# Moving score dots to ScalarE and block updates to VectorE in a residual codebook search

## The chip, the cores and the metric

The kernel runs on one NeuronCore of a Trainium2 chip. The time is the device time of one execution in microseconds. The engines are TensorE (PE, with its weight loads shown apart as PEld), VectorE (DVE), ScalarE (ACT), GpSimd (POOL) and SyncE (SP, which here only issues DMA). Each engine works through its own queue in order; semaphores order the engines among each other. TensorE writes its results to PSUM banks, from which VectorE and ScalarE read.

## The reference

The input is `x` of 2 x 16000 x 512 in bf16. It is a small speech codec: a depthwise convolution of three taps over time, SiLU, four rounds of nearest-codeword search (8 codewords each) on a running residual, and a second depthwise convolution of the chosen codewords' sum.

```python
for i in range(K):                       # K = 3
    z = z + xp[:, i:i+T, :] * dw_enc[i][None, None, :]
z = _silu(z)
res = z
q = jnp.zeros_like(z)
for s in range(Nq):                      # Nq = 4, 8 codewords each
    cb = codebooks[s]
    d2 = einsum(res, res)[..., None] - 2.0 * einsum(res, cb) + einsum(cb, cb)
    idx = d2.argmin(-1)
    sel = cb[idx]
    q = q + sel
    res = res - sel
for i in range(K):
    y = y + qp[:, i:i+T, :] * dw_dec[i][None, None, :]
```

## The kernel before

The 32000 tokens lie as 128 rows of 250 groups, so that one group is 128 tokens, one on each partition. The groups are cut into 17 chunks (`SIZES`, line 27): one of 12, thirteen of 16, two of 12 and one of 6, which is worked on as 8. Channels are on the partitions for most of the work, as four blocks of 128 (`KT` = 4).

For each chunk, `front` runs four blocks. VectorE forms the three tap products (L688) and part of their sums (L696); the other sums are accumulating DMA transfers issued by GpSimd (L694). ScalarE and VectorE alternate for SiLU: exponential (L700), plus one (L704), logarithm (L708), exponential of its negative (L711), and the product into the residual `RES` (L716). `RES` holds the tokens and, between them, columns of the codewords times -2.

Then come four `stage`s, one for each codebook:

- `score` (L769) is TensorE's. For up to six groups at a time it fills one PSUM bank of the pool `psG`, which has two: first a mask (L776), then products of the residual with itself and with the neighbouring codeword columns (L784). The diagonal of the first gives the norm, the columns beside it give eight dots for each token. In a chunk of 16 groups a stage has three such units (6, 6 and 4 groups), in one of 12 two of 6, in the last two of 4: 188 in all.
- `norm` (L804, VectorE) takes the maximum over the masked square, which is the norm. `dots` (L808, VectorE) copies the eight dots of each token from the bank to `PR` and gives the bank back.
- On VectorE the norm is added (L827), then the codewords' norms (L831); the least is taken (L837) and its place marked in the one-hot tile `OH` (L842).
- TensorE turns the one-hots (L853), VectorE copies them (L865), TensorE expands them to pairs (L874), and ScalarE cuts them (`PH`, L883).
- The residual is updated block by block, in one of two ways. For the first `on_dve[s]` blocks TensorE collects the chosen words in `SEL` (`chosen`, L910, six matmuls), and VectorE adds them to `RES` (`subtract`, L920). For the others TensorE builds the whole new residual in `NEW` in two halves (`rest`, L926 and L931), and ScalarE copies each half back (`keep`, L938, or L940 in the smaller chunks). The list `ON_DVE` (line 30) says for each chunk how many blocks of the three updating stages go the first way.

`finish` decodes the one-hots of a chunk into outputs on TensorE (L972); ScalarE copies them out of PSUM (L978), and SyncE issues the stores.

The set-up makes an identity, a mask, the code columns, pair tables and taps. Seven decoder tables are zeroed on VectorE (`taps_of`, L501), filled by DMA from GpSimd's queue (L506) and multiplied by the codewords. Three one-hot tiles are zeroed on VectorE (`presets`, L487). The first chunk's rows are transposed on TensorE (L585) and copied to `XT` for two blocks by ScalarE and for two by VectorE (`move`, L587 to L592).

The order on every engine is written out by a planner (`Plan`, L116). Each piece of work is entered by `plan.add` with its engine, the time it holds it, the time until its result is there, what it needs, a due time, and the slots that it takes and gives (`psG` is the two score banks, `psA` three other PSUM tiles, `Z`, `T`, `E` and so on the SBUF buffers). `run` lists the work forward and backward a few times with shifted ranks (`ROUNDS`) and then shifts ranks by a list of seeds (`MOVES`); the last pass emits the instructions in the order of their planned starts. The planned times order the instructions; on the chip they run when semaphores allow.

Of the kernel before, what the change touches and what calls it, by code (L numbers as in the profile page):

```python
# [14 lines left out]
ACT = mybir.ActivationFunctionType  # L15
# [14 lines left out]
ON_DVE = [(2, 2, 2)] * 3 + [(3, 3, 2)] * 6 + [(3, 3, 3)] * 6 + [(4, 4, 4)] * 2  # L30
# [16 lines left out]
ROUNDS = [(71979, 0.3, 0, 6), (14162, 1, 2, 3), (37709, 0.3, 0, 3), (8398, 0.1, 0.5, 2)]  # L47

MOVES = [403398, 277512, 691281, 942486, 98997, 464427, 609168, 599375, 437497, 903441, 104869, 655643, 319045,
# [59 lines left out]
SWITCH, CLING, SLOW = 0.1, 10.0, 1.08  # L109
# [174 lines left out]
def kernel(  # L284
# [8 lines left out]
    nc = tc.nc  # L293
# [192 lines left out]
    def presets(n):  # L486
        nc.vector.memset(OHB[n], 0.0)  # L487
# [589 lines left out]
```

## Time and profile before

| | |
|---|---|
| median of 3 runs | 682.74 us (680.28 to 682.83) |
| profiled execution | 685.71 us |
| its span, first to last instruction | 683.9 us |
| mean granted TensorE clock | 0.952 |
| busy: VectorE | 637.7 us (93%) |
| busy: ScalarE | 613.0 us (90%) |
| busy: TensorE | 579.5 us (85%) |
| busy: GpSimd | 88.6 us (13%) |

A line of a group says: source line, engine, operation, output <- input with shapes, the number of instructions, then busy time, the mean duration of one in ns, and the engine's idle time just before them with what ended it. Durations of neighbours on one engine overlap, so the distance from one start to the next says what an instruction holds its engine for. In the timeline the columns are start, duration, engine, line, operation. A waits line says who waited for whom, how long in total, how many times, and the longest.

### The profile page before, as it was taken

How to read it: one execution, taken by the hardware profiler on the slowest of the kernel's cores; microseconds unless marked ns; L12 is line 12 of the kernel's file. 1: busy time of each engine (PE TensorE's matmuls, PEld its weight loads, DVE VectorE, ACT ScalarE, POOL GpSimd, SP SyncE). 2: the span in 40 equal slices, each digit the busy share in tenths (PEclk: the TensorE clock that was granted, in tenths of full speed). 3: DMA queues.
4: the chain of work that ended last, by engine and by line, in shares of the span. 5: the costliest groups of instructions: out<-in, count | busy, mean ns of one | idle time of the engine just before them, and what ended most of it. 6: DMA issues, size and time to landing. Idle time of an engine off the chain costs nothing. (4 is left out here: it accounts for less than half of the span.)

```text
span 683.9 us, 25912 instructions
## 1 busy us (share of the span) xinstructions
PE 579.5 (85%) x11637; PEld 332.0 (49%) x11637; DVE 637.7 (93%) x1383; ACT 613.0 (90%) x529; POOL 88.6 (13%) x125
## 2 busy tenths in 40 slices
PE   5056788889989988899888999998988998999995
PEld 5022446454545444454554545554545545556552
DVE  8999999999999989999999999998999999999771
ACT  3589899999999989999999999999999998993556
POOL 6021110110101111110101011101101210010000
PEclk8558899999999999999999999999999999999998
DMA  6999889899698899859898988997679955340335
GB/s 154 179 158 183 151 143 163 167 202 186 126 210 192 150 187 185 186 108 216 211 190 191 170 157 158 192 250 117 146 154 188 187 131 128 97 111 34 126 124 216
DMA packets 162617, 111.55 MB, mean 163 GB/s; under 512 B 143561, under 2 KB 143946, under 8 KB 162378
## 3 DMA queue, kind: packets, MB, share of 16 engines
q1 hardware_dynamic: 150032, 69.88, 45.2%
q0 software_dynamic: 12192, 39.76, 32.3%
q8 instruction: 91, 1.49, 0.9%
q10 hardware_dynamic: 282, 0.26, 0.1%
q14 instruction: 20, 0.16, 0.1%
HBM read 2.39 MB, written 32.77 MB: 51 GB/s over the span
## 5 line engine op out<-in xcount | busy, mean ns | idle before, releaser
L784 PE MATMUL PS<-RES 128*64 128x80 bf16 (+1 forms) x8064 | 175.0, 202 | 10.6 <-DVE RES L716 6.2
L784 PEld LDWEIGHTS <-RES 128*64 128x64 bf16 x8064 | 169.6, 114 | 20.1 <-DVE RES L716 6.8
L920 DVE TENSOR_TENSOR RES<-RES,SEL 128x2048 bf16<-128x2048 bf16 (+2 forms) x183 | 161.3, 910 | 5.4 <-PE SEL L910 5.1
L978 ACT ACTIVATE YSB<-Y 128x1024 bf16<-128x1024 f32 x126 | 127.6, 1037 | 22.8 <-PE Y L972 20.8
L694 POOL DMA_DIRECT2D Z<-T x80 | 73.8, 942 | 510.6 <-DMA XT<-in_x_dram 69.9
L700 ACT ACTIVATE E<-Z 128x2048 bf16<-128x2048 bf16 (+2 forms) x68 | 123.3, 1816 | 9.5 <-DVE Z L696 7.1
L708 ACT ACTIVATE LN<-E 128x2048 f32<-128x2048 bf16 (+2 forms) x68 | 123.1, 1810 | 5.7 <-DVE E L704 4.6
L711 ACT ACTIVATE E<-LN 128x2048 bf16<-128x2048 f32 (+2 forms) x68 | 122.8, 1806 | 0.3
L938 ACT ACTIVATE RES<-NEW 128x1024 bf16<-128x1024 f32 x102 | 104.9, 1053 | 3.6 <-PE NEW L931 3.1
L804 DVE TENSOR_REDUCE TR<-PS 128x6 bf16<-128x384 f32 (+1 forms) x188 | 94.0, 505 | 12.8 <-PE PS L784 12.4
L688 DVE TENSOR_SCALAR T<-XT,WENC 128x2048 bf16<-128x2048 bf16 (+2 forms) x136 | 94.9, 704 | 6.5 <-DMA Z<-T 5.7
L972 PE MATMUL Y<-A,OHT 128*128 128x512 bf16 x249 | 84.6, 386 | 10.3 <-DVE RES L920 5.8
L926 PE MATMUL NEW<-RES,IDENT 128*128 128x512 bf16 (+1 forms) x240 | 71.9, 382 | 10.0 <-ACT RES L938 5.0
L716 DVE TENSOR_TENSOR RES<-Z,E 128x2048 bf16<-128x2048 bf16 (+2 forms) x68 | 77.2, 1136 | 0.2 <-ACT E L711 0.2
L910 PE MATMUL SEL<-PH,HIGH 64*128 64x512 bf16 (+2 forms) x288 | 55.1, 377 | 13.9 <-ACT RES L938 6.0
L776 PE MATMUL PS<-MASK,IDENT 128*64 128x384 bf16 (+1 forms) x376 | 63.3, 333 | 3.6 <-DVE PR L808 3.4
L696 DVE TENSOR_TENSOR Z<-Z,T 128x2048 bf16<-128x2048 bf16 (+2 forms) x56 | 62.5, 1117 | 1.3 <-DMA Z<-T 1.3
L972 PEld LDWEIGHTS <-OHT 128*128 128x128 bf16 x373 | 31.1, 98 | 50.8 <-issue 24.4
L910 PE MATMUL SEL<-PH,MID 64*128 64x512 bf16 (+2 forms) x288 | 52.9, 361 | 0.0
L910 PE MATMUL SEL<-PH,LOW 64*128 64x512 bf16 (+2 forms) x288 | 52.9, 360 | 0.0
L931 PE MATMUL NEW<-PH,EVEN 64*128 64x256 bf16 (+1 forms) x240 | 50.8, 420 | 0.0
L688 DVE TENSOR_SCALAR Z<-XT,WENC 128x2048 bf16<-128x2048 bf16 (+2 forms) x68 | 47.8, 704 | 0.0
(111 smaller groups left out, 617.5 us busy)
## 6 DMA issues: line engine op xcount, KB each, us to landing
Z<-T POOLq DMA_DIRECT2D x65, 512.0 KB, 6.2
out_dram<-YSB SPq DMA_DIRECT2D x61, 512.0 KB, 3.4
Z<-T POOLq DMA_DIRECT2D x10, 384.0 KB, 5.3
RES<-in_x_dram SPq DMA_DIRECT2D x1, 1664.0 KB, 7.2
Z<-T POOLq DMA_DIRECT2D x5, 256.0 KB, 3.7
XT<-in_x_dram SPq DMA_TRANSPOSE x75, 7.1
out_dram<-YSB SPq DMA_DIRECT2D x1, 384.0 KB, 2.4
out_dram<-YSB SPq DMA_DIRECT2D x1, 256.0 KB, 5.4
```

The source lines that it names most:

```text
L688: nc.vector.tensor_scalar(out=places(u[name]), in0=taps(i, k), scalar1=WENC[:, i, k:k + 1], scalar2=None, op0=ALU.mult)
L700: nc.scalar.activation(u["E"][:, 0:G, :], u["Z"][:, 0:G, :], ACT.Exp, scale=-1.0)
L708: nc.scalar.activation(u["LN"][:, 0:G, :], u["E"][:, 0:G, :], ACT.Ln)
L711: nc.scalar.activation(u["E"][:, 0:G, :], u["LN"][:, 0:G, :], ACT.Exp, scale=-1.0)
L716: nc.vector.tensor_tensor(out=tokens(st["RES"], i, G), in0=halves(u["Z"]), in1=halves(u["E"]), op=ALU.mult)
L784: nc.tensor.matmul(V[d * HT:(d + 1) * HT, own - left:own + HT + right], lhsT=row[:, at:at + HT], rhs=row[:, at - left:at + HT + right], st ...
L804: nc.vector.tensor_reduce(out=to, in_=both(u["V", q], m, home, HT), axis=AX.X, op=ALU.max)
L910: nc.tensor.matmul(SEL[:, h, 0:W], lhsT=words[side(h), i * P:(i + 1) * P], rhs=u["PH"][side(h), :], start=(k == 0), stop=(k == len(parts) ...
L920: nc.vector.tensor_tensor(out=old, in0=old, in1=new, op=ALU.add)
L938: nc.scalar.activation(old, new.rearrange("p h (n t) -> p (h n) t", t=HT), ACT.Copy)
L972: nc.tensor.matmul(Y[:, h, :], lhsT=lhs(), rhs=rhs, start=(a == 0), stop=(a == len(terms) - 1))
L978: nc.scalar.activation(u["YSB"][:, k:k + n, :], u[k][:, 0:n, :], ACT.Copy)
```

## The change

Seven things are changed:

- `dots` is a ScalarE copy (an ACTIVATE with Copy) of the same elements from the same bank. It needs the scoring alone, no longer the norm, and the bank is given back when both the norm and the dots are done.
- `ON_DVE` gives 3 blocks of every updating stage to VectorE in chunks 0 to 13 and 4 in chunks 14 to 16. Before, it was 2 in chunks 0 to 2, then (3, 3, 2), then 3, and 4 in the last two chunks.
- All four set-up copies of `move` are ScalarE's.
- `presets` and `taps_of` zero on GpSimd.
- The planner's costs of code columns go from 1.4 (or 1.2) to 0.9, those of the norm from 0.065 to 0.068 a group.
- The planner's costs of TensorE: the turn of one-hots 0.06 to 0.1 (0.13 to 0.1 a tile in the last stage), half a block of `rest` 0.2 to 0.28 plus the same rest, decoding 0.2 to 0.215 a matmul.
- `ROUNDS` and `MOVES`, the seeds, are others, and `MOVES` is longer.

```diff
-ON_DVE = [(2, 2, 2)] * 3 + [(3, 3, 2)] * 6 + [(3, 3, 3)] * 6 + [(4, 4, 4)] * 2
+ON_DVE = [(3, 3, 3)] * 14 + [(4, 4, 4)] * 3
...
-ROUNDS = [(71979, 0.3, 0, 6), (14162, 1, 2, 3), (37709, 0.3, 0, 3), (8398, 0.1, 0.5, 2)]
+ROUNDS = [(46341, 0.3, 0, 4), (76308, 0.1, 2, 3), (32118, 0.1, 0, 1), (72125, 0.1, 0, 1), (12125, 0.3, 0, 1)]
...
     def presets(n):
-        nc.vector.memset(OHB[n], 0.0)
+        nc.gpsimd.memset(OHB[n], 0.0)
...
         t, first, tap, count = PARTS[name]
-        nc.vector.memset(t, 0.0)
+        nc.gpsimd.memset(t, 0.0)
...
-    preset = [plan.add("DVE", 0.3, 0.3 + 0.2, [], early + 2.0 if n == 0 else 0.1 * PERIOD, lambda n=n: presets(n)) for n in range(3)]
+    preset = [plan.add("POOL", 0.5, 0.7, [], early + 2.0 if n == 0 else 0.1 * PERIOD, lambda n=n: presets(n)) for n in range(3)]
...
-            t = plan.add("DVE", 0.2, 0.3, [], (0.3 + 0.02 * n) * PERIOD, lambda name=name: taps_of(name))
+            t = plan.add("POOL", 0.5, 0.7, [], (0.3 + 0.02 * n) * PERIOD, lambda name=name: taps_of(name))
...
-            if i % 2:
-                nc.vector.tensor_copy(st["XT"][:, 0:G + 2, i, :], src)
-            else:
-                nc.scalar.activation(st["XT"][:, 0:G + 2, i, :], src, ACT.Copy)
+            nc.scalar.activation(st["XT"][:, 0:G + 2, i, :], src, ACT.Copy)
...
-            cost = (0.11, 0.07)[i % 2] * (G + 2)
-            st["moved", i] = plan.add(("ACT", "DVE")[i % 2], cost, cost + 0.2, [t], early, lambda i=i: move(i), give=("psA",))
+            cost = 0.11 * (G + 2)
+            st["moved", i] = plan.add("ACT", cost, cost + 0.2, [t], early, lambda i=i: move(i), give=("psA",))
...
-            nc.vector.tensor_copy(to, both(u["V", q], m, code, C).rearrange("p n o c -> p c n o"))
+            src = both(u["V", q], m, code, C).rearrange("p n o c -> p c n o")
+            nc.scalar.activation(to, src, ACT.Copy)
...
-            maxima.append(plan.add("DVE", 0.07 + 0.065 * m, 0.2 + 0.065 * m, [t], due, lambda q=q, m=m: norm(q, m)))
-            maxima.append(plan.add("DVE", 0.06 + 0.01 * m, 0.2, [maxima[-1]], due, lambda q=q, m=m: dots(q, m), give=("psG",)))
+            maxima.append(plan.add("DVE", 0.07 + 0.068 * m, 0.2 + 0.068 * m, [t], due, lambda q=q, m=m: norm(q, m)))
+            maxima.append(plan.add("ACT", 0.11 + 0.007 * m, 0.3, [t], due, lambda q=q, m=m: dots(q, m)))
+            plan.add("FREE", 0.0, 0.0, maxima[-2:], due, lambda: None, give=("psG",))
...
-        hold = 0.13 * MB if last else 0.06
+        hold = 0.1 * MB if last else 0.1
...
-                c = plan.add("PE", 0.2 + 0.65 * f * SLOW, 0.4 + 0.65 * f * SLOW, ready + [st["new"][i, part]], due,
+                c = plan.add("PE", 0.28 + 0.65 * f * SLOW, 0.48 + 0.65 * f * SLOW, ready + [st["new"][i, part]], due,
...
-            d = plan.add("PE", 0.2 * count, 0.2 * count + 0.25, needs, due, lambda k=k: decode(k), take=("psA",))
+            d = plan.add("PE", 0.215 * count, 0.215 * count + 0.25, needs, due, lambda k=k: decode(k), take=("psA",))
```

More of the change, by code (lines that the diff above doesn't have):

```diff
@@ L45 @@
 FAR = -3.3e38
-ROUNDS = [(71979, 0.3, 0, 6), (14162, 1, 2, 3), (37709, 0.3, 0, 3), (8398, 0.1, 0.5, 2)]
-MOVES = [403398, 277512, 691281, 942486, 98997, 464427, 609168, 599375, 437497, 903441, 104869, 655643, 319045,
[55 rows of a table removed]
+ROUNDS = [(46341, 0.3, 0, 4), (76308, 0.1, 2, 3), (32118, 0.1, 0, 1), (72125, 0.1, 0, 1), (12125, 0.3, 0, 1)]
+MOVES = [949848, 17671, 932175, 573655, 719188, 8996, 997728, 468587, 575333, 264370, 591951, 836327, 423319, 577496,
[86 rows of a table added]
 CELLS, COLUMNS, ROWS, QUARTERS = range(4)
@@ L522 @@
     codes = [setup(0.3, 0.5, [ident, book], early, code_words)]
-    codes[0] = plan.add("DVE", 1.4, 1.6, codes, early + 2.0, lambda: code_columns(RESB[0]))
+    codes[0] = plan.add("DVE", 0.9, 1.1, codes, early + 2.0, lambda: code_columns(RESB[0]))
     scored = [plan.add("DVE", 1.3, 1.4, [ident], early + 1.0, mask),
               setup(1.9, 2.1, [ident, book], -0.5 * PERIOD, code_norms)]
-    preset = [plan.add("DVE", 0.3, 0.3 + 0.2, [], early + 2.0 if n == 0 else 0.1 * PERIOD, lambda n=n: presets(n)) for n in range(3)]
+    preset = [plan.add("POOL", 0.5, 0.7, [], early + 2.0 if n == 0 else 0.1 * PERIOD, lambda n=n: presets(n)) for n in range(3)]
     firsts = plan.add("DVE", 1.3, 1.5, [ident], early + 4.0, first_ones)
@@ L534 @@
         words.append(plan.add("DVE", 1.3, 1.5, [t, expanded] + words[-1:], early + 3.0 + s, lambda s=s: pair_words(s)))
-    codes.append(plan.add("DVE", 1.4, 1.6, [codes[0]], 0.1 * PERIOD, lambda: code_columns(RESB[1])))
+    codes.append(plan.add("DVE", 0.9, 1.1, [codes[0]], 0.1 * PERIOD, lambda: code_columns(RESB[1])))
     gate, decoder = [], []
@@ L597, in load_rows @@
                          take=("psA",))
-            cost = (0.11, 0.07)[i % 2] * (G + 2)
-            st["moved", i] = plan.add(("ACT", "DVE")[i % 2], cost, cost + 0.2, [t], early, lambda i=i: move(i), give=("psA",))
+            cost = 0.11 * (G + 2)
+            st["moved", i] = plan.add("ACT", cost, cost + 0.2, [t], early, lambda i=i: move(i), give=("psA",))
             moved.append(st["moved", i])
         st["loaded"] = moved
-        codes.append(plan.add("DVE", 1.2, 1.4, moved + staged + codes[0:1], 0.2 * PERIOD, lambda: code_columns(RESB[2])))
+        codes.append(plan.add("DVE", 0.9, 1.1, moved + staged + codes[0:1], 0.2 * PERIOD, lambda: code_columns(RESB[2])))
         staged.extend(moved)
```

141 rows, old and new, of the table MOVES are left out of this document.

## The prediction

> **What bounds the kernel now.** First the page's head and engine line, then busy time by stretch of the span, then the waits.
>
> ```profile
> span 683.9 us, 25912 instructions
> PE 579.5 (85%) x11637; PEld 332.0 (49%) x11637; DVE 637.7 (93%) x1383; ACT 613.0 (90%) x529; POOL 88.6 (13%) x125
> ```
> ```profile
> 0.00:20.00 20.00, 10.57 (x105) 9.81 (x105) 17.36 (x63) 6.50 (x6) 12.34 (x41) 0.83 0.73 146
> 40.00:60.00 20.00, 13.07 (x147) 6.69 (x147) 19.29 (x38) 18.48 (x17) 2.66 (x3) 0.67 1.08 184
> ...
> 400.00:500.00 100.00, 89.61 (x1853) 50.76 (x1851) 95.91 (x192) 96.07 (x79) 12.60 (x13) 0.97 0.80 167
> 500.00:600.00 100.00, 91.33 (x1964) 53.41 (x1963) 98.06 (x216) 94.72 (x87) 14.82 (x19) 1.00 0.68 151
> 600.00:640.00 40.00, 39.31 (x887) 24.14 (x881) 37.31 (x113) 25.46 (x32) 1.40 (x2) 1.00 0.26 77
> ```
>
> The columns of a stretch are its length, then busy PE, PEld, DVE, ACT and POOL, the granted clock (0.97 to 1.00 late in the span), the DMA share and GB/s. The start is VectorE's. From 400 to 600 VectorE has 194.0 of 200 us and ScalarE 190.8: two engines share the bound, with 6 and 9 us left. From 600 to 640 ScalarE is down to 25.5 of 40, while TensorE has 39.3 and VectorE 37.3. So work taken from VectorE pays everywhere; work put on ScalarE is free only at both ends. What is idle on the two is largely waiting for TensorE:
>
> ```profile
> ACT YSB L978 <- PE Y L972: 20.8, 16, 4.0
> DVE TR L804 <- PE PS L784: 12.4, 16, 2.1
> PEld L776 <- DVE PR L808: 12.4, 22, 1.9
> DVE RES L920 <- PE SEL L910: 5.1, 9, 0.9
> ```
>
> VectorE loses 17.5 us to the scoring and block matmuls; the third row shows the reverse, the next scoring waiting 22 times for a score bank that the dots copy gives back.
>
> **Part 1: dots leave VectorE, blocks come to it.**
>
> ```profile
> L920 DVE TENSOR_TENSOR RES<-RES,SEL 128x2048 bf16<-128x2048 bf16 x105 | 125.9, 1210 | 3.0 <-PE SEL L910 2.9
> L804 DVE TENSOR_REDUCE TR<-PS 128x6 bf16<-128x384 f32 x128 | 69.6, 547 | 7.7 <-PE PS L784 7.5
> L808 DVE CAST PR<-PS 128x48 bf16<-128x48 f32 x128 | 24.8, 196 | 0.0
> L808 DVE CAST PR<-PS 128x32 bf16<-128x32 f32 x60 | 10.7, 179 | 0.0
> ```
> ```profile
> 304.85 1.21 DVE L920 TENSOR_TENSOR RES<-RES,SEL 128x2048 bf16<-128x2048 bf16 x1
> 305.98 0.54 DVE L804 TENSOR_REDUCE TR<-PS 128x6 bf16<-128x384 f32 x1
> ...
> 306.57 0.19 DVE L808 CAST PR<-PS 128x48 bf16<-128x48 f32 x1
> 306.69 0.54 DVE L804 TENSOR_REDUCE TR<-PS 128x6 bf16<-128x384 f32 x1
> ...
> 633.22 1.02 DVE L920 TENSOR_TENSOR RES<-RES,SEL 128x768 bf16<-128x768 bf16 x2
> 634.16 0.26 DVE L837 TENSOR_REDUCE M<-KEY 128x8 bf16<-128x64 bf16 x1
> ```
>
> Rows overlap, so the price of one is the distance to the next start: dots 0.12 us (306.57 to 306.69), a block of a 16-group chunk 1.13, the two halves of a 12-group chunk's block 0.94. Leaving: 128 x 0.12, and 60 x 0.10 for the smaller form, 21.4 us. Coming: the list of blocks sums to 144 before and 162 after, 12 more in 16-group chunks (3 each in chunks 1 and 2, 1 each in 3 to 8) and 6 in 12-group ones (3 each in chunks 0 and 14): 12 x 1.13 + 6 x 0.94 = 19.2. VectorE: **-2.2 us**. By place, chunks 0 to 2 gain VectorE work (3 x 1.13 less 12 x 0.12, some 2 us each), 9 to 13 lose 1.4 each.
>
> **Part 2: ScalarE.**
>
> ```profile
> L938 ACT ACTIVATE RES<-NEW 128x1024 bf16<-128x1024 f32 x102 | 104.9, 1053 | 3.6 <-PE NEW L931 3.1
> L883 ACT ACTIVATE PH<-ps_oh 128x512 bf16<-128x512 f32 x39 | 24.7, 632 | 3.0 <-PE ps_oh L874 3.0
> L940 ACT ACTIVATE RES<-NEW 128x768 bf16<-128x768 f32 x18 | 14.5, 827 | 4.8 <-PE NEW L931 4.7
> L592 ACT ACTIVATE XT<-ps_x 128x1792 bf16<-128x1792 bf16 x2 | 3.3, 1664 | 5.9 <-PE ps_x L585 5.9
> L883 ACT ACTIVATE PH<-ps_oh 128x256 bf16<-128x256 f32 x3 | 1.1, 382 | 0.6 <-PE ps_oh L874 0.6
> ```
> ```profile
> 308.20 0.62 ACT L883 ACTIVATE PH<-ps_oh 128x512 bf16<-128x512 f32 x1
> 308.67 1.05 ACT L938 ACTIVATE RES<-NEW 128x1024 bf16<-128x1024 f32 x1
> 309.58 1.95 ACT L708 ACTIVATE LN<-E 128x2048 f32<-128x2048 bf16 x1
> ```
>
> Each block had two copies here. Leaving: 24 of 0.91 us (308.67 to 309.58) and 12 of about 0.70 (827 ns less the same overlap of 0.14), 30.2 us. Coming: 188 dots, which no row shows on this engine. The two forms of L883 give 0.98 ns an element ((632 - 382) / 256), so a dots of 48 elements would last about 0.18 us by a straight line. If it overlaps as the big ones do, it holds the engine 0.04; if each waits for its matmul and overlaps nothing, 0.18. I take 0.14, nearer the second since each has a TensorE result of its own to await: 188 x 0.14 = 26.3 (ends 7.5 and 34). Two set-up copies come too, 2 x 1.66 less overlap, 3.0. ScalarE: **-0.9 us**, between -20 and +7, not evenly: chunks 9 to 13 get 12 dots each for nothing given back, 1.7 us a chunk.
>
> The Trainium skill, page "ScalarE: Activation LUTs", section "What ACT_TABLE_LOAD costs", gives an ACTIVATE with immediate operands 186 ns plus 0.833 ns an element, and 93 ns of overlap back to back. By it a dots is 0.23 us long and holds the engine 0.13, and the 188 would be 25 us; the rows of 512 and 1024 elements above (632 and 1053 ns) agree with it to 3%, and no run here shows 48 elements.
>
> **Part 3: set-up.**
>
> ```profile
> 24.00 1.08 DVE L590 COPY XT<-ps_x 128x1792 bf16<-128x1792 bf16 x1
> ...
> 25.00 0.60 DVE L688 TENSOR_SCALAR T<-XT,WENC 128x1536 bf16<-128x1536 bf16 x1
> ```
> ```profile
> 6.09 3.92 POOL L451 COPY EXPAND<-LEAST 128x64 bf16<-128x64 bf16 x16 [4.79 <-DVE LEAST L439]
> ...
> 8.07 0.27 DVE L501 MEMSET B<- 128x256 uint32 x1
> ...
> 11.24 0.35 DVE L379 TENSOR_SCALAR CBT<-ps_cbt 128x128 bf16<-128x128 bf16 x2 [0.47 <-PE ps_cbt L377]
> ```
> ```profile
> L501 DVE MEMSET A<- 128x256 uint32 x4 | 1.1, 272 | 0.0
> L633 POOL MEMSET XT<- 128x1024 bf16 x1 | 1.0, 951 | 0.0
> ```
>
> The two XT copies free VectorE of 2 x 1.0 us inside its dense start; ScalarE, busy 6.5 of the first 20 us, hides them, and if it didn't, the fourth block's products would come at most 3.3 us later. Ten memsets of 0.27 (seven tables, three one-hot tiles) are 2.7 us, but the last of them ends at 8.34 us, and at 11.24 VectorE waits for the codebook's transposes anyway: I count 0.5 (ends 0 and 2.7). GpSimd takes them at about half of 951 ns, 4.8 us in all; it idles 4.79 us before its L451 copies. Behind them in its queue stand those copies, the picks, the table fetches and later the accumulating transfers; uncovered, those slip by up to 4.8 us, but the one-hots are first needed when the first score is complete. VectorE: **-2.5 us**.
>
> **Part 4: TensorE, and the new order.**
>
> ```profile
> 308.38 0.39 PE L910 MATMUL SEL<-PH,HIGH 64*128 64x512 bf16 x2 [0.39 <-ACT RES L938]
> ...
> 309.13 0.60 PE L926 MATMUL NEW<-RES,IDENT 128*128 128x512 bf16 x2
> ...
> 310.21 0.60 PE L926 MATMUL NEW<-RES,IDENT 128*128 128x512 bf16 x2
> ```
>
> A block for VectorE costs TensorE 0.75 us (308.38 to 309.13), a block for ScalarE twice 1.08 (309.13 to 310.21). 18 blocks change sides: 12 x 1.41 + 6 x 1.06 = **-23 us** of 579, three blocks of it in chunk 14, near the stretch where TensorE is 98% busy. The planner's cost of a half block was 0.90 and becomes 0.98, nearer to 1.08; decoding goes from 0.20 to 0.215. These are numbers for the planner alone, and with new seeds every engine's order is drawn again. Its worth can only be bounded: between nothing and all of the 17.5 us that VectorE waits for TensorE; the worst, a loss as large, isn't excluded. I take -4: a quarter, since most of TensorE's relief falls on chunks 0 to 2 and 14.
>
> **Part 5: the new waits.** Dots now stand in ScalarE's queue. Behind one that waits for its scoring stand exponentials, logs, block copies and output copies; ahead of it can be an L708 of 1.95 us. The sum of the norms waits for both engines, and so does the bank (two exist): what TensorE lost in 22 waits can grow. The cost is from nothing to half a norm (0.27) on each of 188, 51 us; with a planner that sees these waits I take a tenth of that, **+5**. In the tail the dots lie beside the norms, about -1.
>
> **The sum.** On VectorE -2.2 - 2.5, waits for TensorE -4, new waits +5, tail -1, and 2 to 3 us for ScalarE relieved in chunks 0 to 2 (6 x 0.91 less 1.7, -3.8 a chunk, where its backlog starts): -7. The profiled execution took 685.71 us, 1.8 beyond its span and 3 above the median of 682.74; 682.74 x 678.7 / 685.71 = 675.8, say **676 us**.
>
> **Rivals.** *Nothing gained.* ScalarE becomes the bound in chunks 9 to 13: 190.8 + 5 x 1.7 = 199.3 of the 200 us from 400 to 600. Early relief carries over only through four Z buffers. It gives back 5 to 9 us: 682.
>
> *Norm and dots take turns at a bank.* For it: they read one score bank from two engines, which no row of before shows (PS has L804 and L808 alone, both on VectorE). If the second must wait for the first, whichever engine comes second stands: up to 0.48 us for ScalarE behind a norm, or for VectorE behind a dots that is itself behind a 1.95 us log. The planner gives both the same need, and doesn't know of the turn. Were a third of 188 pairs to collide at 0.3 us, and most of it to show on engines with 3 to 5% to spare, 19 us: 676 + 16 = 692. It decides from 12 us, 0.06 a pair. Against it: both queues are long, so most pairs meet at different times.
>
> The Trainium skill, page "PSUM — Partial Sum Buffer", section "PSUM bank collisions raise a hardware error", speaks for this rival: two engines on one bank and quadrant collide, read against read included, so software has to order them. No row of this trace shows the case.
>
> *The order is much better.* All 17.5 us of VectorE's waits for TensorE go: 665. Against it: the waits shown remain causal, not only badly ordered.
>
> **Chances.** Forecast 0.46 (669 to 680), better order 0.14, nothing gained 0.16, turns at the bank 0.24. What a measurement of this kernel can tell from no change is about 0.5%, 3.4 us: faster 0.59, same 0.15, slower 0.26. The range goes from the better order, 664, to the turns at the bank, 692.
>
> **What would show it.** Right: L808 on ScalarE 188 times at 0.16 to 0.23 us; L920 of 2048 elements 117 times; VectorE near 633 us busy, ScalarE near 612, TensorE near 555; less VectorE waiting for scoring. Wrong: ScalarE idle before dots on VectorE's norms, or VectorE idle before norms and sums on ScalarE's dots, over 12 us together; ScalarE over 99% from 400 to 600; late table fetches.

## The result and the profile after

The changed kernel takes 704.88 us (median; 700.97 to 707.88) against 681.51 us before on the same chip: a ratio of 1.031, 95% interval 1.026 to 1.037. It is 23 us slower where the prediction had 7 us faster, and 13 us above the upper end of the range. Ratios leave out executions over 1.5% above the same kernel's fastest; where times scatter over 20 us that can be half of them or more, so for such kernels the median of all stands beside the ratio.

First the head and the engine line of the page after, to be laid beside the prediction's first fence.

```profile
span 701.1 us, 25688 instructions
PE 564.0 (80%) x11546; PEld 331.0 (47%) x11546; DVE 633.6 (90%) x1207; ACT 606.9 (87%) x683; POOL 92.3 (13%) x135
```

All three large engines have less work than before: VectorE 633.6 us (637.7), ScalarE 606.9 (613.0), TensorE 564.0 (579.5). The span grew by 17.2 us all the same. VectorE's idle time went from 683.9 - 637.7 = 46.2 to 701.1 - 633.6 = 67.5 us: 21.3 more idle, less 4.1 of work, is the 17.2. So none of the three got more work; the added time is idle time. The granted TensorE clock isn't the difference: it was 0.952 in the profiled execution of before and 0.950 in this one.

The groups of instructions, each shape apart, on ScalarE and then on VectorE:

```profile
L837 ACT ACTIVATE PR<-PS 128x48 bf16<-128x48 f32 x128 | 28.1, 221 | 22.2 <-DVE TR L832 15.9 <-PE PS L812 5.6
L837 ACT ACTIVATE PR<-PS 128x32 bf16<-128x32 f32 x60 | 12.5, 210 | 12.8 <-PE PS L812 6.4 <-DVE TR L832 6.3
```
```profile
L950 DVE TENSOR_TENSOR RES<-RES,SEL 128x2048 bf16<-128x2048 bf16 x117 | 140.9, 1219 | 7.3 <-PE SEL L940 7.1
L716 DVE TENSOR_SCALAR T<-XT,WENC 128x2048 bf16<-128x2048 bf16 x104 | 77.5, 751 | 10.9 <-DMA Z<-T 10.9
```

The dots are there 188 times, the large block updates 117 times instead of 105. Behind the bar stands what is new: ScalarE is idle 35.0 us ahead of its dots, nearly as long as the dots themselves last (28.1 + 12.5 = 40.6). The waits of ScalarE and of VectorE (who waited for whom, us in total, times, longest):

```profile
ACT PR L837 <- DVE TR L832: 22.1, 35, 3.4
ACT PR L837 <- PE PS L812: 12.0, 13, 3.3
```
```profile
DVE RES L950 <- PE SEL L940: 12.3, 15, 5.0
DVE T L716 <- DMA Z<-T: 10.9, 3, 7.4
DVE TR L832 <- PE PS L812: 6.6, 12, 1.4
DVE TR L832 <- ACT PR L837: 4.7, 7, 2.3
```

The first row and the last are the turns at a score bank: 35 dots stood behind the norm of the same bank and 7 norms behind the dots, 26.8 us together. VectorE's wait for scoring fell from 12.4 to 6.6 us, but its wait for block matmuls rose from 5.1 to 12.3 and that for accumulating transfers into `Z` from 5.7 (row below) to 10.9. The row of before for that last one:

```profile
DVE T L688 <- DMA Z<-T: 5.7, 5, 2.3
```

How a turn looks in the timeline (start, length, engine, line; in brackets the idle time before it and who ended it). In the first pair the dots wait for the norm, in the second the norm for the dots:

```profile
311.31 0.56 DVE L832 TENSOR_REDUCE TR<-PS 128x6 bf16<-128x384 f32 x1
...
311.90 0.21 ACT L837 ACTIVATE PR<-PS 128x48 bf16<-128x48 f32 x1 [0.43 <-DVE TR L832]
...
319.32 0.25 ACT L837 ACTIVATE PR<-PS 128x48 bf16<-128x48 f32 x1
...
319.61 0.56 DVE L832 TENSOR_REDUCE TR<-PS 128x6 bf16<-128x384 f32 x1 [0.65 <-ACT PR L837]
```

The planner gives the two no order (to it the dots need the scoring alone), yet in neither pair do they run at once: one engine stands until the other has read. That is what the Trainium skill, page "PSUM — Partial Sum Buffer", section "PSUM bank collisions raise a hardware error", demands of software, and the trace agrees: in both brackets the releaser is the other engine's read. Which of the two stands, the order of the program fixes, and not who comes first: in the second pair VectorE stood from 318.96 (319.61 less 0.65), and the dots that it waited for began only at 319.32.

So a turn also hands on whatever made the other engine late. The longest of the 35 waits is of that kind. VectorE had stood 3.38 us for an accumulating transfer, and its norm came late by as much:

```profile
282.78 0.75 DVE L716 TENSOR_SCALAR T<-XT,WENC 128x2048 bf16<-128x2048 bf16 x1 [3.38 <-DMA Z<-T]
...
284.01 0.20 ACT L837 ACTIVATE PR<-PS 128x32 bf16<-128x32 f32 x1 [3.40 <-DVE TR L832]
```

Where the loss sits is seen in busy time by stretch (columns as in the prediction: length, PE, PEld, DVE, ACT, POOL, clock, DMA share, GB/s):

```profile
400.00:500.00 100.00, 81.32 (x1645) 46.85 (x1643) 85.22 (x145) 85.21 (x96) 11.30 (x12) 0.93 0.86 169
500.00:600.00 100.00, 89.12 (x1945) 51.91 (x1941) 97.90 (x182) 94.58 (x113) 13.93 (x18) 1.00 0.63 130
```

From 500 to 600 VectorE is as dense as before (97.9 against 98.1). From 400 to 500 it lost 10.7 us (85.22 against 95.91), half of its 21.3 us of new idle time, and all three engines are less busy there. The timeline there:

```profile
468.82 11.26 SPq L646 DMA_TRANSPOSE XT<-in_x_dram  x4
...
480.88 0.86 POOL L722 DMA_DIRECT2D Z<-T  x1 [14.98 <-DMA XT<-in_x_dram]
...
485.94 0.75 DVE L716 TENSOR_SCALAR T<-XT,WENC 128x2048 bf16<-128x2048 bf16 x1 [7.36 <-DMA Z<-T]
...
487.87 0.61 PE L940 MATMUL SEL<-PH,HIGH 64*128 64x512 bf16 x2 [8.00 <-DVE RES L950]
...
491.42 1.02 ACT L968 ACTIVATE RES<-NEW 128x1024 bf16<-128x1024 f32 x1 [7.70 <-PE NEW L961]
```

GpSimd stood 15 us before its accumulating transfer and was released by the transposing loads of `x`, four of which were issued from 468.82 to 480.08. The transfer was issued at 480.88 and landed some 5 us later; VectorE, next in line for the buffer, stood 7.36 us; TensorE then 8.00 us for VectorE, ScalarE 7.70 for TensorE. One late transfer so holds all three engines in turn, because each queue is in a fixed order. No row of before shows VectorE waiting more than 2.3 us for this transfer.

So two things were on the table: the turns at the bank, which belong to the change, and the order, in which things come late that have nothing to do with dots.

### The profile page after: what moved, and what is told of

The parts are those of the page before. It is cut to its first block, busy times and chain, and to the rows that moved or that the text cites. A ratio compares the mean times of both kernels' runs of the same rounds, so it can differ in the third digit from the quotient of the medians.

```text
span 701.1 us, 25688 instructions
## 1 busy us (share of the span) xinstructions
PE 564.0 (80%) x11546; PEld 331.0 (47%) x11546; DVE 633.6 (90%) x1207; ACT 606.9 (87%) x683; POOL 92.3 (13%) x135
## 5 line engine op out<-in xcount | busy, mean ns | idle before, releaser
L950 DVE TENSOR_TENSOR RES<-RES,SEL 128x2048 bf16<-128x2048 bf16 (+2 forms) x207 | 181.9, 914 | 12.5 <-PE SEL L940 12.3
L812 PE MATMUL PS<-RES 128*64 128x72 bf16 (+1 forms) x8064 | 175.8, 201 | 12.4 <-DVE RES L744 3.9
L716 DVE TENSOR_SCALAR T<-XT,WENC 128x2048 bf16<-128x2048 bf16 (+2 forms) x136 | 96.6, 717 | 10.9 <-DMA Z<-T 10.9
L832 DVE TENSOR_REDUCE TR<-PS 128x6 bf16<-128x384 f32 (+1 forms) x188 | 95.2, 514 | 12.5 <-PE PS L812 6.6
L968 ACT ACTIVATE RES<-NEW 128x1024 bf16<-128x1024 f32 x78 | 79.9, 1034 | 9.5 <-PE NEW L961 9.5
L940 PE MATMUL SEL<-PH,HIGH 64*128 64x512 bf16 (+2 forms) x324 | 63.0, 382 | 27.1 <-DVE RES L950 12.9
L837 ACT ACTIVATE PR<-PS 128x48 bf16<-128x48 f32 (+1 forms) x188 | 39.2, 218 | 35.0 <-DVE TR L832 22.1
L940 PE MATMUL SEL<-PH,MID 64*128 64x512 bf16 (+2 forms) x324 | 61.6, 371 | 0.3 <-DVE MID L510 0.3
L940 PE MATMUL SEL<-PH,LOW 64*128 64x512 bf16 (+2 forms) x324 | 61.2, 369 | 0.3 <-DVE LOW L510 0.3
L956 PE MATMUL NEW<-RES,IDENT 128*128 128x512 bf16 (+1 forms) x168 | 51.4, 388 | 5.9 <-DVE RES L950 3.8
L804 PEld LDWEIGHTS <-IDENT 128*64 128x64 bf16 x376 | 22.9, 108 | 54.7 <-issue 52.6
```

The costliest lines, as they stand in the source:

```text
L716: nc.vector.tensor_scalar(out=places(u[name]), in0=taps(i, k), scalar1=WENC[:, i, k:k + 1], scalar2=None, op0=ALU.mult)
L804: nc.tensor.matmul(both(V[d * HT:(d + 1) * HT], m, home, HT), lhsT=IDENT[:, d * HT:(d + 1) * HT], rhs=MASK[:, 0:m, :].rearrange("p (n o) t ...
L812: nc.tensor.matmul(V[d * HT:(d + 1) * HT, own - left:own + HT + right], lhsT=row[:, at:at + HT], rhs=row[:, at - left:at + HT + right], st ...
L832: nc.vector.tensor_reduce(out=to, in_=both(u["V", q], m, home, HT), axis=AX.X, op=ALU.max)
L940: nc.tensor.matmul(SEL[:, h, 0:W], lhsT=words[side(h), i * P:(i + 1) * P], rhs=u["PH"][side(h), :], start=(k == 0), stop=(k == len(parts) ...
L950: nc.vector.tensor_tensor(out=old, in0=old, in1=new, op=ALU.add)
```

## The experiments

Theory A: the turns of norm and dots at a bank are the loss. Theory B: the new order is the loss, and the same work in another order would show it. Theory C, the prediction's other rival, has ScalarE late because it is fuller.

**Turns taken away in the change's own order.** The dots read a constant SBUF tile and still wait for their scoring's last matmul, so everything keeps its place; the sharing of the bank goes, and the norm alone gives the bank back. The real dots are left out.

```diff
-            src = both(u["V", q], m, code, C).rearrange("p n o c -> p c n o")
-            nc.scalar.activation(to, src, ACT.Copy)
+            src = GWIDE[:, 0:C, place(q):place(q) + m].rearrange("p c (n o) -> p c n o", o=2)
+            t = nc.scalar.activation(to, src, ACT.Copy)
+            tc.add_manual_dep(t.ins, u["S", q].name, ...)
```

> The changed kernel in its own order, but the dots on ScalarE read a constant SBUF tile of the same shape, and wait for the last matmul of their scoring by an added dependency; the score bank is read by the norm alone and given back by it. The kernel so leaves out the real dots, and its outputs are of no use. Theory A (norm and dots take turns at the bank, and that is what costs): no ScalarE wait on a norm is left (22.1 us and 35 times before), none of a norm on a dots (4.7 us), and the time falls from 705 to 685 or less. Theory B (the redrawn order, with its clashes of transfers, is what costs): 698 to 706, with the waits for transfers as they were. Theory C (188 more instructions are simply too much for ScalarE): no change, 703 to 706.

695.38 us, ratio 1.017 (1.010 to 1.024). The waits of ScalarE for norms are gone; VectorE's for block matmuls and for transfers are not (ScalarE's first row, then VectorE's first two):

```profile
ACT PR L837 <- PE PS L812: 16.0, 17, 3.3
```
```profile
DVE RES L952 <- PE SEL L942: 14.8, 17, 6.5
DVE T L716 <- DMA Z<-T: 10.9, 3, 7.3
```

Some ten of the 23 us went with the turns, so of 26.8 us waited at the bank 17 gave nothing. The 7.3 us stall behind the transfer stands as it was, and 12 us remain (695.38 against the 682.98 of before beside it). The gain may be understated, since the stand-in copies are longer than the real dots:

```profile
L837 ACT ACTIVATE PR<-GWIDE 128x48 bf16<-128x48 bf16 x128 | 32.4, 255 | 8.1 <-PE PS L812 7.8
```

With 14.3 us for the smaller form that is 46.7 us against 40.6. The runs below that take the dots off the bank have the same stand-in.

**The same work in other orders.** Only the ranks by which the planner lists the work are replaced, by those of a search from other seeds; the instructions are the same.

```diff
-ROUNDS = [(46341, 0.3, 0, 4), (76308, 0.1, 2, 3), (32118, 0.1, 0, 1), (72125, 0.1, 0, 1), (12125, 0.3, 0, 1)]
-MOVES = [949848, 17671, 932175, 573655,
...
+RANKS = [
...
     def run(self):
...
+        self.emit(*self.pass_over(RANKS))
```

> The changed kernel as it is, but for its order, which is drawn again by a search of the same kind with other seeds, to a planned length within 1 us of its own. Theory A: the turns come back whatever the draw, ScalarE waits 15 to 30 us on norms, and the time is 695 to 712. Theory B: the time depends on the draw, and lies anywhere between 680 and 715; below 690 would speak for B.

> The changed kernel's work in the second drawn order, for comparison on one chip with its version off the bank: 1.01 to 1.02 of before, 690 to 697 us.

> The changed kernel's work in a third drawn order (planned length 666.4 us, where its own order has 662.9 and the second 663.9). If the turns at the bank are a price of the change whatever the order, ScalarE waits 15 to 30 us for norms again and the time is 1.01 to 1.04 of before. If the loss was only the luck of the drawn order, one order in three should come near 1.00.

The second order took 694.69 us, 1.016 (1.009 to 1.023), and on another chip 694.80, 1.020 (1.016 to 1.024). The third took 700.42, 1.028 (1.024 to 1.032). So 4 to 10 us lie between orders of one and the same work, and none of three comes near 1.00. The turns are in all of them. ScalarE's row of the third order:

```profile
ACT PR L1010 <- DVE TR L1005: 19.3, 30, 2.7
```

**Turns taken away in those orders.** The edit is the one above.

> The changed kernel in the other drawn order, in which it took 695, but the dots read a constant SBUF tile as in the first experiment, so that the two readers take no turns (the real dots are left out). The first experiment gave 9.5 us for that; its share here should be near what this order's trace shows of it, 16.3 us of ScalarE waiting on norms and 6.0 of VectorE waiting on dots, in part hidden: 685 to 690. Were the turns a small matter beside the draw: 692 to 695.

> The second order with the dots off the bank (the real dots are left out). Its ten times lay in two groups, 680 to 686 and 691 to 703. If the turns are worth 12 us in this order, most lie near 681; if removing them only lets the kernel fall on good days, the two groups stand again and the median is some 6 us under the run before.

> The third order with the dots reading a constant SBUF tile after their scoring's last matmul (the real dots are left out). If the turns are worth some 10 us in every order of the changed kernel: 8 to 13 us less than the run before. If what they are worth hangs on the order, as it did when before's own order gave nothing: within 4 us of it.

In the second order this took 688.58 us the first time (ratio 0.998, 0.994 to 1.003), by the ratios 12 us less and all of the loss. Its ten times were in two groups, 680 to 686 and 691 to 703, so it was run again beside its version with turns: 695.80 us (683.92 to 710.44; ratio 1.011, 1.005 to 1.017) against 694.80. By the medians of all executions removing the turns gave 6 us one time and nothing the other, by the ratios 12 and 6; it widened the scatter. In the third order the gain is 694.97 against 700.42, 5 us (ratio 1.018 against 1.028). Over the three orders the turns cost, by the medians, 10, 5 and 0 to 6 us. Theory A so holds for a part of the loss, some half of it or less; the second order's ratios and the longer stand-in leave room for more, and no run sets a firm bound.

**Dots on ScalarE in before's order.** One line of before is changed, its planned order stays.

```diff
-            nc.vector.tensor_copy(to, both(u["V", q], m, code, C).rearrange("p n o c -> p c n o"))
+            nc.scalar.activation(to, both(u["V", q], m, code, C).rearrange("p n o c -> p c n o"), ACT.Copy)
```

> The kernel before in its own order on every engine, with one change: each dots copy is issued to ScalarE at the place where it stood on VectorE. Nothing is planned anew, no block moves. VectorE has 21 us less, ScalarE 20 to 28 more. Theory A: the turns cost in a good order too; ScalarE waits 15 us or more on norms and TensorE on dots, and the time is 690 to 705. Theory B: in its good order it holds, 680 to 690. Theory C (ScalarE is full): over 700, with ScalarE busy over 98% from 100 to 600.

> As the kernel before with only its dots on ScalarE (which took 696), but the dots read a constant SBUF tile and wait for the last matmul of their scoring by an added dependency; the real dots are left out. Nothing else differs, the order neither. If the turns at the bank are the cost there too: 682 to 688, with no ScalarE wait on norms (12.6 us before). If it is that ScalarE comes to its dots late whoever reads the bank (VectorE waited 19.8 us for them before the sum), 692 to 697.

The first took 696.30 us, 1.018 (1.012 to 1.023); with the dots off the bank it was 699.93, 1.025 (1.022 to 1.028): no gain. VectorE's waits in the first, then in the second:

```profile
DVE TR L804 <- PE PS L784: 22.9, 33, 2.1
DVE V L827 <- ACT PR L808: 19.8, 31, 1.6
```
```profile
DVE V L830 <- ACT PR L809: 25.8, 34, 1.8
DVE TR L804 <- PE PS L784: 13.9, 20, 2.1
```

VectorE dropped all 188 copies and adds the norm to dots that ScalarE hasn't made yet: 20 to 26 us of waits, with or without the bank. Here ScalarE got the dots and gave no block back, and the order wasn't planned for them; theory C fits, and so does an order that suits the work badly. In the change's own order that wait is only 1.5 us, so this case isn't the cause there.

**The planner told of the turn.** The dots need the norm in the plan (`[maxima[-1]]` instead of `[t]`), and a new order is drawn.

> The changed kernel, with one need changed in the planner: the dots need the norm, as the software makes the second reader of a bank wait; the order is drawn again with that. Theory A: ScalarE's waits on norms fall below 8 us, and the time to 680 to 692, since the planner no longer puts the two side by side. Theory B: the time is that of any newly drawn order of this work, 695 to 710. Theory C: over 700, ScalarE being full.

709.91 us, 1.042 (1.035 to 1.049), the worst of the changed kernels, with one wait of 7.4 us among 22:

```profile
ACT PR L1011 <- DVE TR L1006: 30.6, 22, 7.4
```

In the plan too the dots now come second. On the chip ScalarE then stands fewer times (22 against 35), and its longest wait grew from 3.4 to 7.4 us. The trace shows where that one comes from: again VectorE stood for an accumulating transfer, and the norm behind it was late.

```profile
483.05 0.76 DVE L890 TENSOR_SCALAR T<-XT,WENC 128x2048 bf16<-128x2048 bf16 x1 [7.38 <-DMA Z<-T]
...
484.30 0.21 ACT L1011 ACTIVATE PR<-PS 128x48 bf16<-128x48 f32 x1 [7.44 <-DVE TR L1006]
```

**The rest of the change without its dots.** Dots back on VectorE, `ON_DVE` as before; set-up and planner costs stay as changed; order drawn anew.

```diff
-ON_DVE = [(3, 3, 3)] * 14 + [(4, 4, 4)] * 3
+ON_DVE = [(2, 2, 2)] * 3 + [(3, 3, 2)] * 6 + [(3, 3, 3)] * 6 + [(4, 4, 4)] * 2
...
-            nc.scalar.activation(to, src, ACT.Copy)
+            nc.vector.tensor_copy(to, src)
```

> The changed kernel with the dots back on VectorE behind the norm and the list of blocks of before; set-up copies, zeroing on GpSimd and the planner's costs for TensorE stay changed; the order is drawn again. Theory A: all that cost is gone, and what is left of the change is worth 0 to 6 us: 676 to 684. Theory B: 695 or more, since the planner's new costs or a new draw are at fault.

700.22 us, 1.025 (1.019 to 1.030): no turns, no dots on ScalarE, and still 17 us lost. That is theory B's case, with the set-up and the TensorE costs as suspects beside the order. The set-up alone, in before's order (copies of `XT` to ScalarE, zeroing to GpSimd):

```diff
-        nc.vector.memset(OHB[n], 0.0)
+        nc.gpsimd.memset(OHB[n], 0.0)
...
-        nc.vector.memset(t, 0.0)
+        nc.gpsimd.memset(t, 0.0)
...
-                nc.vector.tensor_copy(st["XT"][:, 0:G + 2, i, :], src)
```

> The kernel before in its own order on every engine, with the set-up part of the change alone: the two XT copies go to ScalarE and the ten zeroings to GpSimd, at the places where they stood. The prediction's price for it was 2.5 us: 677 to 681. If those copies were no bound, 681 to 684.

682.43 us, 1.002 (0.999 to 1.004): nothing, in either direction.

**Before's work in other orders.** None of the change; only the ranks are replaced, as above. The last has the change's TensorE costs in the planner besides.

> The kernel before, work unchanged, but its order drawn again by a search of the same kind with other seeds, to a planned length within 1 us of its own. Theory B, in its sharp form (an order drawn by the planner alone is worth what chance gives it on the chip, and the order of the kernel before was a good one): 690 to 705, although nothing of the change is in it. Theory A (turns at the bank and nothing else): 679 to 686, since dots and norms are both on VectorE.

> The work of before, none of the change, in another drawn order (planned length 667.6 us, where its own order has 666.6). If any drawn order loses some 12 us against the order that before has: 1.010 to 1.020 of before. If a new order costs nothing by itself and the second draw (1.0107) was a bad one: 0.996 to 1.006.

> The work of before in a further drawn order, less long sought (planned length 670.8 us). If any drawn order loses some 12 us against the order that before has: 1.010 to 1.025. If new orders scatter on both sides of before's: within 1% of it either way.

> The work of before, with the change's costs for TensorE in the planner and nothing else of it, in a drawn order (planned length 672.7). If the traced times give better orders: at or under the other draws of before's work, 0.995 to 1.008. If they do nothing: like those, 1.010 to 1.020.

| work | order | median us | ratio (95%) |
|---|---|---|---|
| before | its own | 681 to 684 | 1 |
| before | second | 693.05 | 1.011 (1.000 to 1.021) |
| before | third | 702.25 | 1.013 (1.005 to 1.021) |
| before | fourth | 711.48 | 1.039 (1.034 to 1.043) |
| before | traced TensorE costs | 700.23 | 1.022 (1.016 to 1.027) |
| after | its own | 704.88 | 1.031 (1.026 to 1.037) |
| after | second | 694.7, 694.8 | 1.016, 1.020 |
| after | third | 700.42 | 1.028 (1.024 to 1.032) |

This speaks for theory B as the larger part. Four other orders of before's work, with no dots moved, lose 1 to 4%, though for the second and the third the interval reaches down to 1.000 and 1.005. Three orders of the changed work lose 2 to 3%. The median of before's three other orders with its own costs averages 702 us, that of the changed work's three 700: the scatter from order to order (18 and 10 us) hides any difference between the two works. What the profile of before's fourth order shows is the picture of the changed kernel, without the change. Head and engine line, then VectorE's waits:

```profile
span 705.7 us, 25862 instructions
PE 576.7 (82%) x11574; PEld 337.6 (48%) x11647; DVE 641.8 (91%) x1383; ACT 612.2 (87%) x529; POOL 87.0 (12%) x125
```
```profile
DVE TR L993 <- PE PS L973: 16.2, 25, 1.4
DVE T L877 <- DMA Z<-T: 13.1, 4, 8.4
DVE RES L1109 <- PE SEL L1099: 6.6, 10, 2.6
```

Idle is 705.7 - 641.8 = 63.9 us, against 46.2 in before's own order and 67.5 after the change. Again a few waits for an accumulating transfer are long, 13.1 us in 4 with one of 8.4. In the third order they are 16.7 us, in the one with traced costs 13.5:

```profile
DVE T L878 <- DMA Z<-T: 16.7, 8, 5.0
```
```profile
DVE T L878 <- DMA Z<-T: 13.5, 8, 5.6
```

The traced TensorE costs didn't give a better order than the old ones (700 us, within 693 to 711). The planner's own reckoning tells little. Before's orders with its own costs end by the plan at 666.6 us (its own), within 1 us of that (the second), 667.6 and 670.8, and took 682 to 684, 693, 702 and 711: the times rise with the plans, but 1 us more of plan went with 18 us on the chip, and 4 with 28. The changed work's three end at 662.9 (its own), 663.9 and 666.4 and took 705, 695 and 700: there the best by the plan is the slowest.

**Two suspects within the change's order.** First the transfers. Transposing loads and accumulating transfers take turns: each waits for the second last issued of the other kind (`LAG` = 2). Here it waits for the third last.

```diff
-LAG, SLACK, STORE = 2, 4.5, 0.35
+LAG, SLACK, STORE = 3, 4.5, 0.35
```

> The changed kernel in its own order, but an accumulating transfer waits for the third-last transposing load before it and not the second-last, and the other way round (LAG 3 for 2). Theory B: VectorE's stalls on accumulating transfers (3.4 us near 280 and 7.4 near 482) shrink to a half or less, and the time falls by 5 to 10, to about 696. Theory A: they are not what costs, 702 to 706. If the two kinds of transfer hinder each other when let closer, it gets slower instead, over 707.

707.50 us, 1.030 (1.021 to 1.039). The long wait for `Z` stays, in the longest of its four executions, which is the profiled one:

```profile
DVE T L716 <- DMA Z<-T: 13.6, 3, 8.2
```

The transfer was issued at 482.16 and VectorE went on at 491.95: this time the landing itself was late, beside transposing loads. So loosening these turns gains nothing; whether the two kinds of transfer slow each other down otherwise is open. Second, TensorE itself stands 5.3 us in the middle of a run of expansion matmuls of which all have what they need:

```profile
159.73 0.29 PE L904 MATMUL ps_oh<-MT,EXPAND 128*128 128x64 bf16 x4
...
165.34 0.80 PE L904 MATMUL ps_oh<-MT,EXPAND 128*128 128x64 bf16 x12 [5.32 <-issue]
...
167.57 1.22 DVE L950 TENSOR_TENSOR RES<-RES,SEL 128x2048 bf16<-128x2048 bf16 x1 [5.04 <-PE SEL L940]
```

The last line is VectorE's longest wait for block matmuls, 5.0 of the 12.3 us: it follows from this.

To see whether TensorE's standstill hangs on the place in TensorE's program, 64 more idle matmuls are put ahead of everything:

```diff
-        for _ in range(AHEAD):
+        for _ in range(AHEAD + 64):
```

> The changed kernel in its own order with 64 more idle matmuls at the start, where TensorE waits for set-up anyway, so that every later TensorE instruction lies 128 further on in the program. In the changed kernel, and in the two runs in its order, TensorE stood still for 5.3 to 6.6 us in the middle of the 16 expansion matmuls near 160 us, waiting for nothing that the profile shows. If that is TensorE's program arriving late while transposing loads hold the DMA engines, the gap moves to another instruction and may shrink: 698 to 706, no gap over 3 us between those 16 matmuls. If it belongs to those matmuls and what they read, it stays where it is.

703.70 us, 1.030 (1.026 to 1.034). The same 16 matmuls then run without a gap,

```profile
157.91 0.65 PE L904 MATMUL ps_oh<-MT,EXPAND 128*128 128x64 bf16 x16
```

and another gap, of 4.2 us, opens elsewhere, in the middle of a scoring:

```profile
PE PS L812 <- issue: 5.1, 4, 4.2
```

So the gap doesn't belong to these matmuls, and moving it gains nothing that can be measured. TensorE's matmul waits for which the profile names no cause are 8.8 us in all in the change's order and 1.8 in before's. But the order of before's work with traced costs has 1.7 us of them, the rest of the change without its dots 0.9, and both lost 16 to 17 us. So they aren't what most of a new order's loss is made of.

## Why the prediction was wrong

*The work.* These terms held, TensorE's by two thirds. VectorE 633.6 us (predicted near 633), ScalarE 606.9 (near 612), TensorE 564.0 (near 555). The dots last 0.21 to 0.22 us, inside 0.16 to 0.23. Their price was too high: where ScalarE has one ready, the next instruction starts 0.09 us later:

```profile
306.04 0.21 ACT L837 ACTIVATE PR<-PS 128x48 bf16<-128x48 f32 x1
306.13 1.04 ACT L1008 ACTIVATE YSB<-Y 128x1024 bf16<-128x1024 f32 x1
```

At 0.09 the 188 cost 17 us and not 26; ScalarE came out 5 us under the forecast. TensorE gave back 15.5 of the 23 us.

*The set-up*, -2.5 us: measured alone it is worth nothing (1.002). The start of VectorE did get emptier, 12.5 of the first 20 us against 17.4, but its wait there for the codebook's transposes grew from 0.5 to 5.7 us.

*The new waits*, +5: the mechanism was named as a rival, "norm and dots take turns at a bank", with a third of 188 pairs at 0.3 us, 19 us waited and 16 shown. The runs have 42 pairs at 0.64 us, 26.8 us waited and, by the medians, 0 to 10 us shown. Its cap of 0.48 us behind a norm was wrong: the longest wait is 3.4, because the program fixes who goes first and the norm itself can be late. Its own mark of 12 us idle was passed, and it still isn't the larger half: the argument "most of it shows on engines with 3 to 5% to spare" failed; that an engine which waits at the bank would mostly have waited a little later for something else fits, and is argued, not measured. The other part of the new waits, ScalarE late with the dots, was mentioned and priced inside the 5; with before's order kept it is the largest new wait (19.8 and 25.8 us), with a loss of 14 to 17 us, but in the changed kernel it is 1.5. And the "22 waits" that TensorE was said to lose at the banks are those of its weight loads; its matmuls stood there 3.4 us in 7 waits before, and 5.1 in 10 after (3.4 for norms, 1.7 for dots).

*The new order*, -4: this is the step that failed. It was bounded by "all of the 17.5 us that VectorE waits for TensorE" as a gain and "a loss as large", and taken as a quarter of the gain, since TensorE was relieved. What it should have asked is how good before's order is among orders: with the planner's price of an order unknown, 4 us of gain had no run behind it. Four other orders of before's work cost 11 to 28 us more by their medians (693, 702, 700 and 711 against the 682 to 684 of the runs beside them), and none less. The change replaces the order, so a loss of that kind was to be expected whatever the work. The prediction treated the order as a small correction to a sum of work, and drew its price from the waits that it might remove. One of them did shrink, VectorE's for scoring, by 5.8 us; those for block matmuls and for transfers grew by 7.2 and 5.2, and ScalarE got 35.0 us of waits at its dots that had no row before. The sum's -1 for the tail and its 2 to 3 us for ScalarE's relief were measured by no run alone.

*The rivals.* None of the three was right as told. "Turns at the bank" had the right sign and named a true part of the mechanism, but the time, 704.9, is beyond its 692, since most of the rest is the order. "Nothing gained" let ScalarE bound the stretch from 400 to 600; it was busy there 179.8 of 200 us, less than before.

Open is why before's own order is 11 to 28 us better than four others. The traces show where others lose (long waits for transfers and for scoring), not why that one doesn't, and how its seeds were chosen among others is not on record. Whether an order of the changed work exists that beats before isn't known: of three, none does, and no kernel run here beats before.

## What to carry to other kernels

Where the order of the work is drawn by a planner, an edit that redraws it is two changes: price the new order by itself, by drawing the old work again a few times, before any sum of work is trusted to 1%. A planner's end time is a poor measure among good orders (of the changed work's three, the shortest plan, by 3.5 us, ran 4 us longer than the longest). And a wait seen in the trace is a bound on what its removal gives, not the gain: 26.8 us of turns were worth 0 to 10 by the medians, and the longest of them were other delays handed on.

## What the runs showed of the hardware

- A ScalarE copy of 48 elements a partition out of PSUM is 0.22 us long and holds the engine 0.09 us when its input is ready (306.04 to 306.13 above); out of an SBUF tile in bf16 it was 0.255 us long in the same order. The Trainium skill, page "ScalarE: Activation LUTs", section "What ACT_TABLE_LOAD costs", gives 186 ns plus 0.833 ns an element and 93 ns of overlap, by estimate 0.23 and 0.13 us; the trace agrees on the length and has the hold shorter.
- TensorE can stand 4 to 5 us ahead of matmuls that wait for nothing the trace shows; the place moves with the program when 64 matmuls are put ahead of it. Waiting for its own code, with five transposing loads issued over 18 us around it, would fit; no run shows that. The Trainium skill, page "Runtime: NRT & Kernel Launch", section "Instruction fetch mechanics", calls such fetches mostly hidden.
- Two engines that read one PSUM bank take turns in the order that the program fixes, so the second also waits while the first is late: up to 3.4 us for a norm of 0.42 us.
- An accumulating transfer of 512 KB lands in 5.6 us by its median, and in one case beside four transposing loads VectorE got on only 9.8 us after the issue (482.16 to 491.95).
- One kernel whose instructions don't change (the second order with the dots off the bank) ran from 680.5 to 702.9 us on one chip and from 683.9 to 710.4 on another, where the kernel before stayed within 678 to 690 beside it. Four executions would have told a wrong story.
